# A two-layer memory-attention kernel: the last two segments projected as one, and other places for work in the one-layer steps

## The chip, the core and the metric

The kernel runs on one core of one Trainium2 chip. The metric is the device time of one execution in microseconds (us), the median of several runs. The core has a matrix engine (TensorE, PE in the profile; its weight loads are PEld), a vector engine (VectorE, DVE), a scalar engine (ScalarE, ACT), GpSimd (POOL) and a queue engine for transfers (SyncE, SP). Each engine works through a list of instructions of its own; semaphores join the lists. Matrix products land in the accumulation memory PSUM, from where DVE or ACT copies them into the main buffer.

## The reference

```python
# x: 2048 x 448; mem0: 8 x 448; 16 heads of 256; segments of 32 tokens
def _A_ref(x, mem0, Wq, Wk, Wv, Wo, seg_len):      # attention with a memory
    mem = mem0
    for s in range(n_seg):                          # 64 segments, in order
        h = concatenate([mem, x[segment s]])        # 8 + 32 tokens
        q, k, v = h @ Wq, h @ Wk, h @ Wv            # per head
        p = softmax(where(mask, q @ k.T * scale, -1e9))
        o = (p @ v) @ Wo
        mem = o[:M]                                 # the next segment's memory
        outs.append(o[M:])
def _B_ref(x, W_gate, W_up, W_down):                # feed-forward, 448 -> 1792 -> 448
    gate = x @ W_gate
    return (gate * (gate > 0) * (x @ W_up)) @ W_down
x = x + _A_ref(layernorm(x), ...)
x = x + _B_ref(layernorm(x), ...)
x = x + _A_ref(layernorm(x), ...)
x = x + _B_ref(layernorm(x), ...)
```

Both layers use the same weights. Each layer is a chain: a segment's memory is needed before the next segment's scores.

## The kernel before

**Preparation (to about 69 us).** The weights come in, are transposed on PE and multiplied out: A_sb holds the products of query and key weights, B_sb those of value and output weights. So a step needs no separate q, k, v or output product. `idle` (L322 to L329) adds 32 and 16 transposes of the identity that nothing reads.

**Steps.** `step(g, ff)` (L599 to L838) runs for g = 0 to 68. It holds segment g of layer 1 (chain c = 0, g up to 63) and segment g - 4 of layer 2 (c = 1, g from 4 to 67). So steps 0 to 3 and 64 to 67 have one chain, the "one-layer steps", and 60 steps have two. A step's stages, by the names in the profile:

- prj: hT (the normalized tokens and memory, transposed) times A_sb, into PSUM banks that `open_banks` and `close_bank` (L508 to L546) open and copy to TQ and TZ, the queries. Heads come in two halves, hf = 0 and 1; the banks are named b0 to b3 with z0 and z1 for the first half, c0 to c3 for the second.
- Sm and Sx: scores of the memory's 8 queries (`scores_m`, L621) and of the 32 tokens (`scores_x`, L629). `weights_begin` and `weights_end` (L554 to L571) turn them into probabilities PM and PX: mx, se, ssum, rs on DVE with the exponential on ACT.
- flips: PE transposes the probabilities, pps in whole (`flipped`, L573) or ppr in row halves (`flipped_rows`, L581), and DVE (ACT for one half of the rows) copies them to PT.
- weighting: `weigh_m` (L644, products ya and yb) for the memory's first half, `weigh_m_rows` (L657, ym) for its second, `weigh_x` (L673, y) for the tokens. The results go to Y (first half of the heads) and Z (second half). The memory's are used in the same step, the tokens' in the next.
- projection: `project_out` (L703) multiplies B_sb with Y and Z into one PSUM bank ox, 168 matmuls a step; `project_tail` (L714) does the last 64 output dimensions in 56 matmuls o, in column pairs, rows 0 to 63 and 64 to 127 of one bank. So step g projects the memory of step g and the tokens of step g - 1. Step 68 has no chain and only projects the tokens of segment 63 of layer 2. `finish` (L736) copies ox into the next memory and into OT, the tokens' output.

**Feed-forward.** The class `Feed` (L408 to L478) handles a block of 64 tokens of layer 1 (rows 64 to 127) and one of layer 2 (rows 0 to 63) at once. It runs at odd g from 3 on, 33 times inside a step, and once after the loop (L852 to L859). In steps 3 and 5 there is no layer-2 block yet; in step 67 and after the loop no layer-1 block is left. Its parts: `residual` (flips OT to otp, adds, statistics), `norm` (rstd on POOL, then xn; L769 asks for POOL, after the loop DVE does it), `xposed` (four transposes tps, copies to xT), `gate_up(u)` for u = 0 to 6 (28 matmuls ups and gps each, ut on ACT, hh on DVE), `down` (14 matmuls dps and the add), `norm2` and `feed_on` (the normalized block goes to layer 2) and `leave` (layer 2's block is stored).

**What sets the order.** The order on PE is written by hand: `mm`, `tr` and `in_order` (L71 to L85) tie each matmul to the one before in program order. The orders of DVE, ACT, POOL and SP follow from a scheduler. The pool "ps" has seven PSUM banks, handed around by all tags; ox has the eighth. A matmul that opens a bank waits for the reader of its former content.

In a one-layer step the middle goes like this (L793 to L800), before `project_out` fills the time in which the probabilities are made:

```python
            Sx0 = scores_x(0)
            if ff is not None:
                ff.xposed()
            scores_m(1)
            Sx1 = scores_x(1)
            pm = flipped(PM[0], 1, "m0")
            weigh_m(0, hk, pm)
            probs_x(0, Sx0)
```

Of the kernel before, what the change touches and what calls it, by code (L numbers as in the profile page):

```python
# [8 lines left out]
BF = mybir.dt.bfloat16  # L9
# [44 lines left out]
def build_kernel(ctx, tc, A_x, A_mem0, A_Wq, A_Wk, A_Wv, A_Wo, B_W_gate, B_W_up, B_W_down, out,  # L54
# [29 lines left out]
    def tr(*a):  # L84
        in_order(nc.tensor.transpose(*a))  # L85
# [119 lines left out]
        nc.vector.tensor_copy(mem_cols(g, cs)[:, 0:n], src)  # L205


    with tc.tile_pool(name="pre", bufs=3) as pre:
        mem0_n = pre.tile([MEM, 512], BF, name="mem0_n", bufs=1)
        nc.gpsimd.dma_start(mem0_n[:, 0:DM], mem0)  # L210
# [108 lines left out]
            load_next()  # L319
            return transposed(nat[i], i == 0)  # L320

        warm = psum.tile([P, 2 * DM], BF, tag="ps", name="warm")  # L322
        def idle(n):
            for _ in range(n):
                tr(warm[:, 0:128], ident[:], ident[:])

        idle(32)
        cur = flip_next(0)
        idle(16)  # L329
# [67 lines left out]
    nc.vector.memset(OT[:], 0.0)  # L397
    xT = main.tile([P, NPASS, 128], BF, name="xT")
    hh = main.tile([P, FT, 128], BF, name="hh")
    nc.gpsimd.memset(hh[:], 0.0)  # L400
    HK = []
    for i in range(2):
# [5 lines left out]
    class Feed:  # L408


        def __init__(self, i):
            self.i = i
            self.first = i < nblk
            self.second = 0 <= i - LAG // BLK < nblk
            self.n = slice(0 if self.second else TB, P if self.first else TB)
            self.x = xa[i % 3]
            self.nx = xp[i % 2]

        def residual(self):
            tp = flipped_dims("otp", lambda r, kd: OT[ROWS[r], kd, :])  # L420
# [7 lines left out]

        def xposed(self):
            tps = transpose_tokens(self.xn)  # L430
            nc.vector.tensor_copy(xT[:, 0:4, :], tps[:])
            for r in range(2):
                nc.scalar.copy(xT[ROWS[r], 4:NPASS, :], tps[ROWS[1 - r], 0:3, :])  # L433

        def gate_up(self, u):
            n = self.n
# [13 lines left out]
        def down(self):  # L450
            i = self.i
            dps = self.dps = psum.tile([P, 512], F32, tag="ps", name="dps")
            for f in range(FT):
                mm(dps[:, 0:DM], hh[:, f, :], Wd_sb[:, f, :], start=(f == 0), stop=(f == FT - 1))
            if self.first:
                nc.vector.tensor_tensor(self.nx[TB:P, :], dps[TB:P, 0:DM], self.x[TB:P, :], op=ALU.add)
                self.st = row_stats(self.nx)
                nc.sync.dma_start(xa[(i + 2) % 3][0:TB, :], self.nx[TB:P, :])
                if i + 3 < nblk:
                    nc.sync.dma_start(self.x[TB:P, :], x_dram[block(i + 3)])  # L460

        def norm2(self):
            if self.first:
# [4 lines left out]
        def leave(self):  # L468
            i = self.i
            if self.second:  # L470
                nc.vector.tensor_tensor(self.x[0:TB, :], self.dps[0:TB, 0:DM], self.x[0:TB, :], op=ALU.add)
                nc.sync.dma_start(out_dram[block(i - LAG // BLK)], self.x[0:TB, :])

        def feed_on(self):
# [103 lines left out]
        nc.vector.tensor_copy(PT[:], pps[:].rearrange("p b q -> p (b q)"))  # L578
        return PT

    def flipped_rows(srcs):  # L581

        blocks = [src[:, 2 * b:2 * b + 2, :] for src, n in srcs for b in range(n)]
        n = len(blocks)
        two = [psum.tile([P, n, 64], BF, tag="ps", name=f"ppr{r}") for r in range(2)]
        for b, src in enumerate(blocks):
            for r in range(2):
                tr(two[r][:, b, :], src[ROWS[r]], ident[ROWS[r], ROWS[r]])
        PT = main.tile([P, n * 128], BF, tag=f"PTr{n}", name="PT")
        for r, eng in enumerate((nc.vector, nc.scalar)):  # L590
            evac(eng, PT[:].rearrange("p (b r q) -> p b r q", r=2, q=64)[:, :, r, :], two[r][:])
        return PT

# [5 lines left out]
    def step(g, ff):  # L599
# [4 lines left out]
        hb = hTb[gb % 2]  # L604
        cols = [(0, 32) if c == 0 else (48, 80) for c in xs] + [(32, 40) if c == 0 else (40, 48) for c in ms]
        lo, hi = min(a for a, _ in cols), max(b for _, b in cols)
        ox = None

        def ys(hf, later=0):
# [62 lines left out]

        def weigh_x(hf, hk, PT):  # L673

            def keep(eng, c, t0, src):
                n = src.shape[-1] // SEG
                dst = ys(hf, 1)[:, t0:t0 + n, XO[c]:XO[c] + SEG]
                k = max(1, n // 8)
                evac(eng, dst.rearrange("p (k i) (e q) -> p k e i q", k=k, q=16),
                     src.rearrange("p (k e i q) -> p k e i q", k=k, e=2, q=16))  # L680

            y1 = {c: psum.tile([P, 512], F32, tag="ps", name=f"y1_{c}") for c in chains}
            for kd in range(2):
                for c in chains:
                    rows = slice(64 * c, 64 * c + L)
                    mm(y1[c][:, kd * 256:kd * 256 + 256], hk[rows, kd, :], PT[rows, 0:256], start=True, stop=True)
            for c in chains:
                keep(nc.scalar if c == 0 else nc.vector, c, 0, y1[c][:])
            y2 = {c: psum.tile([P, 512], F32, tag="ps", name=f"y2_{c}") for c in chains}
            for kd in (2, 3):  # L690
                for c in chains:
                    rows = slice(64 * c, 64 * c + L)
                    mm(y2[c][:, kd * 256 - 512:kd * 256 - 256], hk[rows, kd, :], PT[rows, 0:256], start=True, stop=True)
            for c in chains:
                keep(nc.scalar if c == 0 else nc.vector, c, 16, y2[c][:, 0:256])
                tail = y2[c][:, 256:512].rearrange("p (o e i q) -> p e i o q", o=2, e=2, i=4)
                for e in range(2):
                    rows = slice(64 * e, 64 * e + 64)
                    evac(nc.vector if c == 0 else nc.scalar,
                         ys(hf, 1)[rows, 24:28, XO[c]:XO[c] + SEG].rearrange("p i (o q) -> p i o q", q=16),  # L700
                         tail[rows, e])

        def project_out(hf, t0, t1):  # L703

            nonlocal ox
            if ox is None:
                ox = psum.tile([P, 3, W], F32, tag="ox", bufs=1, name="ox")
            for t in range(t0, t1):
                for mc in range(3):
                    mm(ox[:, mc, lo:hi], B_sb[:, hf, t, mc * 128:(mc + 1) * 128],  # L710
                       ys(hf)[:, t, lo:hi], start=(hf == 0 and t == 0 and mc == 0),
                       stop=(hf == 1 and t == NT - 1 and mc == 2), skip_group_check=True)

        def project_tail():  # L714

            o3 = psum.tile([P, W], F32, tag="ps", name="o3")
            for hf in range(2):
                for t in range(0, NT, 2):
                    for e in range(2):
                        mm(o3[64 * e:64 * e + 64, lo:hi], B_sb[:, hf, t + e, 384:DM], ys(hf)[:, t + e, lo:hi],  # L720
                           start=(hf == 0 and t == 0), stop=(hf == 1 and t == NT - 2))
            nc.scalar.copy(swap[0:64, lo:hi], o3[64:128, lo:hi])
            nc.scalar.copy(swap[64:128, lo:hi], o3[0:64, lo:hi])
            if ms:
                both = slice(M0 + MEM * ms[0], M0 + MEM * (ms[-1] + 1))
                nc.vector.tensor_tensor(mem_cols(g + 1, ms)[:, 3], o3[:, both].rearrange("p (c m) -> p c m", m=MEM),
                                        swap[:, both].rearrange("p (c m) -> p c m", m=MEM), op=ALU.add)
            for c in xs:
                x = slice(XO[c], XO[c] + SEG)
                nc.vector.tensor_tensor(ot_cols(c)[:, 3], o3[:, x], swap[:, x], op=ALU.add)  # L730

        def ot_cols(c):
            o = (g - 1) % BLK * SEG + (TB if c == 0 else 0)
# [2 lines left out]
        def finish():  # L736
            if ms:
                src = ox[:, :, M0:M0 + 16].rearrange("p k (c m) -> p k c m", m=MEM)
                set_mem(g + 1, src[:, :, ms[0]:ms[-1] + 1, :], ms, 3)
            for c in xs:  # L740
                nc.scalar.copy(ot_cols(c)[:, 0:3], ox[:, :, XO[c]:XO[c] + SEG])

        def feed(*us):
            if ff is not None:
# [21 lines left out]
        close_bank(b2, chains, hb, j, nc.scalar)  # L766
        if ff is not None:
            ff.residual()
            ff.norm(nc.gpsimd)  # L769
        b1, b3, z0, z1 = open_banks(chains, hb, j, (0, 1), (0, 3), (0, 4), (1, 4))  # L770
        close_bank(z0, chains, hb, j, None)
        load_some()
# [6 lines left out]
        close_bank(c0, chains, hb, j, nc.scalar)  # L779
        close_bank(c2, chains, hb, j, nc.scalar)  # L780
        close_bank(c1, chains, hb, j, nc.vector)
        close_bank(c3, chains, hb, j, nc.scalar)
        if len(chains) == 2:
            pm = flipped(PM[0], 1, "m0")
# [6 lines left out]
            probs_x(0, Sx0)  # L791
        else:
            Sx0 = scores_x(0)  # L793
            if ff is not None:
                ff.xposed()
            scores_m(1)
            Sx1 = scores_x(1)
            pm = flipped(PM[0], 1, "m0")
            weigh_m(0, hk, pm)
            probs_x(0, Sx0)  # L800
        if g < 2:
            load_some()
        if ff is not None:
# [47 lines left out]

    ff = Feed(nblk + LAG // BLK - 1)  # L852
    ff.residual()
    ff.norm()
    ff.xposed()
    for u in range(FT // 2):
        ff.gate_up(u)
    ff.down()
# [59 lines left out]
```

## Time and profile before

| what | value |
|---|---|
| median of 3 runs | 1584.73 us (1580.89, 1584.73, 1585.72) |
| the profiled execution | 1579.01 us, its span 1576.9 us |
| PE busy | 1547.3 us, 98% of the span |
| PEld, DVE, ACT, POOL busy | 90%, 71%, 50%, 11% |
| mean granted clock of TensorE | 0.993 |
| ACT copies OT <- ox | 128, 24.8 us |
| DMA | 33.12 MB, mean 21 GB/s |

The profile's page is one execution as the hardware profiler saw it. It gives each engine's busy time, then the span in 40 slices with tenths of busy time and of the granted clock, then the chain of waits that ended last, then groups of instructions. A group's line names the source line, the engine, the operation, output <- input, the shape and the count; then come busy us and mean ns of one, and behind the second bar the idle us of the engine just before them with what ended it. PE's mean ns is one instruction's latency, and neighbours overlap; a rate comes from busy us over the count. The timeline's lines give start and duration in us and, in brackets, the wait before. Counts of the form 128*64 are rows times columns of the matrix engine in use.

### The profile page before, as it was taken

The numbers are of one execution on the slowest core, as the hardware profiler recorded it, in microseconds if no ns is written. First come the engines' busy times: TensorE is split into PE (matmuls) and PEld (weight loads), VectorE is DVE, ScalarE is ACT, GpSimd is POOL, SyncE is SP. The second block draws the span as 40 slices with busy tenths as digits, with TensorE's granted clock in tenths as the row PEclk, the third lists the DMA queues.
The fourth block names the chain that finished last, engine by engine and source line by source line (L and its number), as shares of the span: only waits on it lengthen the run. The fifth ranks groups of instructions, "written<-read, shape, count | busy, mean of one in ns | idle before, by whom it ended". The sixth has DMA issues, their size and how long they took to land.

```text
span 1576.9 us, 98176 instructions
## 1 busy us (share of the span) xinstructions
PE 1547.3 (98%) x45116; PEld 1422.8 (90%) x45116; DVE 1112.7 (71%) x3825; ACT 783.3 (50%) x2307; POOL 174.9 (11%) x308
## 2 busy tenths in 40 slices
PE   8999999999999999999999999999999999999997
PEld 6588899999999999999999999999999999999886
DVE  6756777777777777777767677776777777776673
ACT  6634544554445544544445545554455545544442
POOL 3201111011001111011001111011011110111010
PEclk9989999999999999999999999999999999999999
DMA  9530000000000000000000000000000000000000
GB/s 285 149 80 9 9 10 8 6 10 10 10 10 10 10 10 8 6 9 10 10 10 10 10 10 5 8 10 10 10 10 10 10 10 5 9 8 7 7 7 6
DMA packets 29468, 33.12 MB, mean 21 GB/s; under 512 B 3320, under 2 KB 28160, under 8 KB 29056
## 3 DMA queue, kind: packets, MB, share of 16 engines
q1 hardware_dynamic: 28992, 26.85, 6.3%
q8 instruction: 352, 5.77, 1.5%
q14 instruction: 60, 0.49, 0.1%
q0 software_dynamic: 64, 0.01, 0.0%
HBM read 23.18 MB, written 1.84 MB: 16 GB/s over the span
## 4 chain that ended last, share of the span: by engine, by line
PE 94%; DVE 2%; ACT 1%; POOL 1%; issue 1%; DMA 0%; SPq 0%; POOLq 0%; ACTq 0%; DVEq 0%
PE prj L82 29%; PE ox L82 25%; PE ups L82 10%; PE dps L82 6%; PE o L82 5%; PE y L82 4%; PE Sx L82 3%; PE Sm L82 2%; PE bps L82 1%; PE pps L85 1%; PE gps L82 1%; PE aps L82 1%; PE tps L85 1%; PE kps L85 1%; PE ym L82 1%
## 5 line engine op out<-in xcount | busy, mean ns | idle before, releaser
L82 PEld LDWEIGHTS <-B_sb 128*128 128x128 bf16 (+1 forms) x15456 | 495.0, 103 | 29.2 <-issue 21.2
L82 PE MATMUL prj<-hT,A_sb 128*128 128x80 bf16 (+1 forms) x11424 | 430.6, 200 | 0.0
L82 PEld LDWEIGHTS <-A_sb 128*128 128x128 bf16 x11424 | 406.3, 100 | 8.3
L82 PE MATMUL ox<-Y,B_sb 128*128 128x80 bf16 (+4 forms) x5880 | 222.9, 199 | 1.9 <-DVE Y L650 1.9
L89 ACT CAST TQ<-prj 128x480 bf16<-128x480 f32 (+1 forms) x380 | 183.1, 494 | 82.8 <-PE prj L82 58.6
L82 PE MATMUL ox<-Z,B_sb 128*128 128x80 bf16 (+2 forms) x5712 | 217.7, 199 | 1.3 <-DVE Z L650 1.3
L82 PE MATMUL ups<-xT,Wgu_sb 64*128 64x128 bf16 (+1 forms) x3332 | 190.8, 214 | 1.3 <-DVE hh L447 0.8
L82 PE MATMUL gps<-xT,Wgu_sb 64*128 64x128 bf16 (+1 forms) x3332 | 190.9, 214 | 0.4 <-ACT xT L433 0.3
L82 PEld LDWEIGHTS <-Wgu_sb 64*128 64x128 bf16 x6664 | 179.1, 95 | 4.5 <-issue 2.5
L91 DVE CAST TQ<-prj 128x480 bf16<-128x480 f32 (+1 forms) x228 | 129.5, 574 | 17.3 <-PE prj L82 11.7
L447 DVE SCALAR_TENSOR_TENSOR hh<-gps,ut 128x256 bf16<-128x256 f32 (+1 forms) x238 | 94.7, 408 | 47.7 <-ACT ut L446 34.7
L446 ACT CAST ut<-ups 128x256 bf16<-128x256 f32 (+1 forms) x238 | 85.5, 359 | 82.1 <-PE gps L82 63.4
L89 ACT CAST Y<-y 64x128 bf16<-64x128 f32 (+2 forms) x256 | 89.4, 379 | 45.6 <-DVE Y L91 41.4
L91 DVE CAST Y<-y 64x128 bf16<-64x128 f32 (+2 forms) x256 | 102.1, 419 | 13.3 <-ACT Y L89 4.3
L89 ACT COPY hT<-tps 128x256 bf16<-128x256 bf16 x32 | 11.9, 372 | 197.8 <-DVE hT L91 197.8
L91 DVE CAST Z<-y 64x128 bf16<-64x128 f32 (+2 forms) x256 | 99.1, 418 | 12.4 <-ACT Z L89 5.5
L578 DVE COPY PT<-pps 128x128 bf16<-128x128 bf16 (+1 forms) x206 | 49.9, 256 | 80.3 <-PE pps L85 77.6
L89 ACT CAST Z<-y 64x128 bf16<-64x128 f32 (+2 forms) x256 | 89.2, 378 | 23.9 <-DVE Z L91 17.4
L89 ACT CAST TZ<-prj 64x320 bf16<-64x320 f32 (+2 forms) x152 | 56.1, 380 | 86.7 <-DVE TZ L91 78.7
L171 POOL TENSOR_SCALAR rstd<-mv 128x1 f32<-128x1 f32 x67 | 15.2, 227 | 729.2 <-DVE mv L169 729.2
L566 DVE TENSOR_REDUCE ssum<-se 128x2 f32<-128x80 f32 (+1 forms) x270 | 70.8, 274 | 35.7 <-ACT se L560 33.5
L82 PE MATMUL dps<-Wd_sb,hh 128*128 128x448 bf16 x476 | 96.0, 353 | 0.0
(130 smaller groups left out, 2342.1 us busy)
## 6 DMA issues: line engine op xcount, KB each, us to landing
wo<-in_A_Wo_dram SPq DMA_DIRECT2D x8, 448.0 KB, 7.7
nat<-in_A_Wq_dram SPq DMA_DIRECT2D x8, 384.0 KB, 6.2
nat<-in_A_Wk_dram SPq DMA_DIRECT2D x8, 384.0 KB, 6.4
nat<-in_A_Wv_dram SPq DMA_DIRECT2D x8, 384.0 KB, 7.2
xa<-in_A_x_dram SPq DMA_DIRECT2D x32, 56.0 KB, 2.8
xa<-xp SPq DMA_DIRECT2D x32, 56.0 KB, 1.9
out_dram<-xa SPq DMA_DIRECT2D x32, 56.0 KB, 2.0
xp<-in_A_x_dram SPq DMA_DIRECT2D x30, 56.0 KB, 2.1
```

The costliest lines, as they stand in the source:

```text
L82: in_order(nc.tensor.matmul(*a, **k))
L85: in_order(nc.tensor.transpose(*a))
L89: nc.scalar.copy(dst, src)
L91: eng.tensor_copy(dst, src)
L171: nc.gpsimd.tensor_scalar(out=rstd[:], in0=mv[:, 1:2], scalar1=EPS, scalar2=None, op0=ALU.add)
L446: nc.scalar.copy(ut[:, :, n], ups[:, :, n])
L447: nc.vector.scalar_tensor_tensor(out=hh[:, 2 * u:2 * u + 2, n], in0=gps[:, :, n], scalar=0.0, in1=ut[:, :, n], op0=ALU.max, op1=ALU.mult)
L566: nc.vector.tensor_reduce(ssum[:], se[:], axis=AX.X, op=ALU.add)
L578: nc.vector.tensor_copy(PT[:], pps[:].rearrange("p b q -> p (b q)"))
```

## The change

Parts, in the order of the diff:

1. `idle` becomes a function that takes a PSUM bank of its own at each call; the 32 and 16 transposes of the preparation stay. After the loop `idle(44)` stands between `residual` and `norm`, `idle(12)` between `xposed` and `gate_up`.
2. `xposed` copies only the 64 token columns that exist when the block has one half.
3. `down` for such a block (steps 3, 5, 67 and after the loop) takes 64 columns of hh as weights and writes even f to rows 0 to 63 and odd f to rows 64 to 127 of dps. `sum_up` then adds the two halves and x: a copy on ACT and two adds on DVE, instead of one add.
4. `weigh_x` in step 67 writes segment 63's y beside segment 62's, into the same buffers. Step 67 then projects nothing and only feeds, flips and weighs; step 68 projects 64 columns, both segments at once. 224 matmuls (168 ox, 56 o) are gone.
5. `finish` copies the second segment's OT on DVE instead of ACT. This holds in all 60 two-layer steps too, and once in step 68.
6. In one-layer steps `norm` runs on DVE; the memory flip `pm` comes right behind the first `scores_x`, `weigh_m` between `scores_m(1)` and the second `scores_x`, and `xposed` between the closes of banks c1 and c3. In step 67 there is no memory flip.

In the built kernel's lists, PE has 15232 loads of B_sb (15456 before), 56 dps matmuls of 64 rows beside 420 of 128 (476 before) and 104 idle transposes (48). DVE has 61 copies OT <- ox (0) and ACT 67 (128). In the two-layer steps the OT copy stands on DVE behind the first copy of y. In steps 3 and 65 DVE's list has both xn ahead of the last queries' copies TQ of bank b1, for which the memory scores Sm of the first half wait. Two early loads change places on SP. PE's list in the two-layer steps is the same.

```diff
+    def idle(n):
+        warm = psum.tile([P, 128], BF, tag="ps", name="warm")
+        for _ in range(n):
+            tr(warm[:], ident[:], ident[:])
...
+            self.both = self.first and self.second
...
         def xposed(self):
             tps = transpose_tokens(self.xn)
-            nc.vector.tensor_copy(xT[:, 0:4, :], tps[:])
+            n = self.n
+            nc.vector.tensor_copy(xT[:, 0:4, n], tps[:, :, n])
             for r in range(2):
-                nc.scalar.copy(xT[ROWS[r], 4:NPASS, :], tps[ROWS[1 - r], 0:3, :])
+                nc.scalar.copy(xT[ROWS[r], 4:NPASS, n], tps[ROWS[1 - r], 0:3, n])
...
             for f in range(FT):
-                mm(dps[:, 0:DM], hh[:, f, :], Wd_sb[:, f, :], start=(f == 0), stop=(f == FT - 1))
+                if self.both:
+                    mm(dps[:, 0:DM], hh[:, f, :], Wd_sb[:, f, :], start=(f == 0), stop=(f == FT - 1))
+                else:
+                    mm(dps[ROWS[f % 2], 0:DM], hh[:, f, self.n], Wd_sb[:, f, :], start=(f < 2), stop=(f >= FT - 2))
...
+        def sum_up(self, dst, o):
+            n = slice(o, o + TB)
+            if self.both:
+                nc.vector.tensor_tensor(dst[n, :], self.dps[n, 0:DM], self.x[n, :], op=ALU.add)
+                return
+            nc.scalar.copy(part[n, 1, :], self.dps[TB - o:P - o, 0:DM])
+            nc.vector.tensor_tensor(part[n, 0, :], self.dps[n, 0:DM], self.x[n, :], op=ALU.add)
+            nc.vector.tensor_tensor(dst[n, :], part[n, 0, :], part[n, 1, :], op=ALU.add)
...
+        last = g == nseg + LAG - 1
+        now = 0 if chains else 1
+        if not chains:
+            lo -= SEG
+
+        def outs():
+            if not chains:
+                return [(lo, OT[:, :, SEG:TB]), (lo + SEG, OT[:, :, 0:SEG])]
+            return [(XO[c], ot_cols(c)) for c in xs]
...
+            kept, xo = (ys(hf), (None, XO[1] - SEG)) if last else (ys(hf, 1), XO)
...
-            for c in xs:
-                nc.scalar.copy(ot_cols(c)[:, 0:3], ox[:, :, XO[c]:XO[c] + SEG])
+            for k, (x, ot) in enumerate(outs()):
+                evac(nc.vector if k else nc.scalar, ot[:, 0:3], ox[:, :, x:x + SEG])
...
-            ff.norm(nc.gpsimd)
+            ff.norm(nc.gpsimd if len(chains) == 2 else None)
...
         close_bank(c1, chains, hb, j, nc.vector)
+        if ff is not None and len(chains) == 1:
+            ff.xposed()
         close_bank(c3, chains, hb, j, nc.scalar)
...
             Sx0 = scores_x(0)
-            if ff is not None:
-                ff.xposed()
+            pm = flipped(PM[0], 1, "m0") if ms else None
             scores_m(1)
+            weigh_m(0, hk, pm)
             Sx1 = scores_x(1)
-            pm = flipped(PM[0], 1, "m0")
-            weigh_m(0, hk, pm)
             probs_x(0, Sx0)
+        if last:
+            probs_x(1, Sx1)
+            feed(0, 1, 2, 3)
+            px0 = flipped_rows([(PX[0], 2)])
+            feed(4)
+            weigh_x(0, hk, px0)
+            feed(5)
+            px1 = flipped_rows([(PX[1], 2)], "x1")
+            feed(6)
+            weigh_x(1, hk, px1)
+            ff.down()
+            ff.leave()
+            return
...
     ff.residual()
+    idle(44)
     ff.norm()
     ff.xposed()
+    idle(12)
```

More of the change, by code (lines that the diff above doesn't have):

```diff
@@ L320, in flip_next @@
             return transposed(nat[i], i == 0)
[L322 to L325, printed above, removed]
         idle(32)
@@ L399, in build_kernel @@
     hh = main.tile([P, FT, 128], BF, name="hh")
+    part = main.tile([P, 2, DM], F32, name="part")
     nc.gpsimd.memset(hh[:], 0.0)
@@ L453, in down @@
             for f in range(FT):
-                mm(dps[:, 0:DM], hh[:, f, :], Wd_sb[:, f, :], start=(f == 0), stop=(f == FT - 1))
+                if self.both:
+                    mm(dps[:, 0:DM], hh[:, f, :], Wd_sb[:, f, :], start=(f == 0), stop=(f == FT - 1))
+                else:
+                    mm(dps[ROWS[f % 2], 0:DM], hh[:, f, self.n], Wd_sb[:, f, :], start=(f < 2), stop=(f >= FT - 2))
             if self.first:
-                nc.vector.tensor_tensor(self.nx[TB:P, :], dps[TB:P, 0:DM], self.x[TB:P, :], op=ALU.add)
+                self.sum_up(self.nx, TB)
                 self.st = row_stats(self.nx)
@@ L470, in leave @@
             if self.second:
-                nc.vector.tensor_tensor(self.x[0:TB, :], self.dps[0:TB, 0:DM], self.x[0:TB, :], op=ALU.add)
+                self.sum_up(self.x, 0)
                 nc.sync.dma_start(out_dram[block(i - LAG // BLK)], self.x[0:TB, :])
@@ L579, in flipped, with flipped_rows @@
         return PT
-    def flipped_rows(srcs):
+    def flipped_rows(srcs, tag=""):
         blocks = [src[:, 2 * b:2 * b + 2, :] for src, n in srcs for b in range(n)]
@@ L588, in flipped_rows @@
                 tr(two[r][:, b, :], src[ROWS[r]], ident[ROWS[r], ROWS[r]])
-        PT = main.tile([P, n * 128], BF, tag=f"PTr{n}", name="PT")
+        PT = main.tile([P, n * 128], BF, tag=f"PTr{n}{tag}", name="PT")
         for r, eng in enumerate((nc.vector, nc.scalar)):
@@ L673, in weigh_x @@
         def weigh_x(hf, hk, PT):
+            kept, xo = (ys(hf), (None, XO[1] - SEG)) if last else (ys(hf, 1), XO)
             def keep(eng, c, t0, src):
                 n = src.shape[-1] // SEG
-                dst = ys(hf, 1)[:, t0:t0 + n, XO[c]:XO[c] + SEG]
+                dst = kept[:, t0:t0 + n, xo[c]:xo[c] + SEG]
                 k = max(1, n // 8)
@@ L699, in weigh_x @@
                     evac(nc.vector if c == 0 else nc.scalar,
-                         ys(hf, 1)[rows, 24:28, XO[c]:XO[c] + SEG].rearrange("p i (o q) -> p i o q", q=16),
+                         kept[rows, 24:28, xo[c]:xo[c] + SEG].rearrange("p i (o q) -> p i o q", q=16),
                          tail[rows, e])
@@ L710, in project_out @@
                     mm(ox[:, mc, lo:hi], B_sb[:, hf, t, mc * 128:(mc + 1) * 128],
-                       ys(hf)[:, t, lo:hi], start=(hf == 0 and t == 0 and mc == 0),
+                       ys(hf, now)[:, t, lo:hi], start=(hf == 0 and t == 0 and mc == 0),
                        stop=(hf == 1 and t == NT - 1 and mc == 2), skip_group_check=True)
@@ L719, in project_tail @@
                     for e in range(2):
-                        mm(o3[64 * e:64 * e + 64, lo:hi], B_sb[:, hf, t + e, 384:DM], ys(hf)[:, t + e, lo:hi],
+                        mm(o3[64 * e:64 * e + 64, lo:hi], B_sb[:, hf, t + e, 384:DM], ys(hf, now)[:, t + e, lo:hi],
                            start=(hf == 0 and t == 0), stop=(hf == 1 and t == NT - 2))
@@ L727, in project_tail @@
                                         swap[:, both].rearrange("p (c m) -> p c m", m=MEM), op=ALU.add)
-            for c in xs:
-                x = slice(XO[c], XO[c] + SEG)
-                nc.vector.tensor_tensor(ot_cols(c)[:, 3], o3[:, x], swap[:, x], op=ALU.add)
+            for x, ot in outs():
+                nc.vector.tensor_tensor(ot[:, 3], o3[:, x:x + SEG], swap[:, x:x + SEG], op=ALU.add)
         def ot_cols(c):
@@ L739, in finish @@
                 set_mem(g + 1, src[:, :, ms[0]:ms[-1] + 1, :], ms, 3)
-            for c in xs:
-                nc.scalar.copy(ot_cols(c)[:, 0:3], ox[:, :, XO[c]:XO[c] + SEG])
+            for k, (x, ot) in enumerate(outs()):
+                evac(nc.vector if k else nc.scalar, ot[:, 0:3], ox[:, :, x:x + SEG])
         def feed(*us):
```

## The prediction

> **What bounds the kernel now.** I read the table of slices first, then the chain of waits, then PE's waits by line, then the end in order of time. From the page:
>
> ```profile
> PE   8999999999999999999999999999999999999997
> PEclk9989999999999999999999999999999999999999
> ...
> PE 94%; DVE 2%; ACT 1%; POOL 1%; issue 1%; DMA 0%; SPq 0%; POOLq 0%; ACTq 0%; DVEq 0%
> ...
> L82 PE MATMUL dps<-Wd_sb,hh 128*128 128x448 bf16 x476 | 96.0, 353 | 0.0
> ```
>
> TensorE is busy at full clock in every slice but the last, and 94% of the chain is its own work. Here time goes only if matmuls go or if PE waits less. The last line's 96.0 us over 476 is 200 ns for a down matmul (the 353 beside it is one instruction's latency), so the 14 of one block take 2.8 us. Where PE waits, by its groups:
>
> ```profile
> L82 PE MATMUL ya<-PT,hk 128*128 128x128 bf16 x134 | 18.2, 217 | 2.7 <-DVE PT L578 2.7
> ...
> L82 PE MATMUL ox<-Z,B_sb 128*128 128x40 bf16 x504 | 14.4, 180 | 1.3 <-DVE Z L650 1.3
> ```
>
> With 1.9 us of the same kind for `ox<-Y`, and 0.5 us at `pps`, these are the one-layer steps: seven stalls of 0.43 to 0.54 us before ya and seven of 0.50 to 0.62 us before ox. In the two-layer steps PE hardly waits. The end, in order of time:
>
> ```profile
> 1556.41 4.38 PE L82 MATMUL ox<-Y,B_sb 128*128 128x32 bf16 x168
> ...
> 1561.12 0.29 PE L85 MATMUL otp<-ident,OT 64*128 64x64 bf16 x8 [0.33 <-ACT OT L741]
> ...
> 1564.24 0.61 PE L85 MATMUL tps<-ident,xn 128*128 128x128 bf16 x4 [2.82 <-DVE xn L181]
> ...
> 1565.35 0.97 ACT L433 COPY xT<-tps 64x384 bf16<-64x384 bf16 x2 [4.28 <-DVE xT L431]
> ...
> 1570.35 2.82 PE L82 MATMUL dps<-Wd_sb,hh 128*128 128x448 bf16 x14
> 1573.20 0.62 DVE L471 TENSOR_TENSOR xa<-dps,xa 64x448 bf16<-64x448 f32 x1 [2.21 <-PE dps L82]
> ```
>
> The last segment's projection and the last feed-forward block stand alone here. In this stage the granted clock is 1.00 until 1562, 0.57 in 1562 to 1564.2, 0.50 until 1569 and 0.95 after. So gate-up takes 4.85 us (1565.37 to 1570.2).
>
> **The change part by part.** Base: the profiled execution, 1579.01 us (span 1576.9 and 2.1 around it), 5.7 under the median of 1584.73. I subtract the sum from both.
>
> *End, steps 67 and 68.* Removed from step 67: 168 ox matmuls of 32 columns at 26.5 ns (4.45 us) and 56 o at about 22 ns (1.23 us). Step 68's ox grows to 64 columns: 40 columns cost 27.5 ns and 80 cost 36, between them about 32, so 168 x 5.5 ns = +0.9. Its o tail costs 20 to 22 ns at any width shown: 0. Down in pairs: 14 matmuls in 7 slots of 200 ns, -1.4. Work: -4.45 - 1.23 + 0.9 - 1.4 = -6.2. PE's waits in 1539 to 1556.4 are 0.31 + 0.27 + 0.65 + 0.93 + 0.26 = 2.4 us. The removed projection covered the softmax, the Z copies and the hh products; now only gate-up (28 matmuls of 64 columns, 0.41 us a call) and flips stand between them. With the order of the changed build I put its durations behind each other: the second scores wait 0.3 for queries on ACT; gate-up calls 3 and 4 wait 0.5 each for ut and hh; y waits 0.3 for its flip, the second y 1.0, since ACT copies a flip only behind the Z tails. That is 2.6, so -6.0. Bounds: all waits hidden, -8.6; each y copied with nothing beside it (Z copies 1.02 + 0.53, twice, 3 more), -3.0.
>
> *Last block.* OT is now copied for two segments, ACT (0.24) then DVE, which waits for ACT: +0.27. idle(44) runs while residual and norm run; a warm transpose took 55 ns at the start, so 2.4 of the 2.82 us wait is filled. idle(12), 0.66 us, lies beside the xT copies. xT narrower: DVE 0.43 to about 0.27; ACT's two 0.97 to about 0.6. At full clock the 196 gate-up matmuls take 14.7 ns (0.41/28). The first 17 need DVE's half, ready 0.16 earlier; the others wait for ACT until 0.6 after, and 179 x 14.7 = 2.6 more: 3.3 against 4.85 from a start 0.16 earlier, -1.7. Pairs -1.4. The sum of two halves is serial: ACT copy (0.53, the row of the 128x448 copy), DVE add, DVE add (about 0.6): +1.1. Sum -1.7; if the clock drops all the same, -0.4; if ACT's copies hide, -2.8.
>
> *Other down projections* (steps 3 and 5). Step 5: -1.4, and the chain of sum, statistics and xn, 1.1 longer, still ends where DVE reached xn before (185.71, rstd done at 184.43, tps at 186.54). Step 3: -1.4, but there xn (143.62) followed rstd (143.37) at once and tps at 144.06 had no slack: +0.8. The pairs' price is bounded by 0 (no overlap) and -1.4; I take -1.4, since in the preparation four aps matmuls of half width (128*64, 384 columns) last 0.52 us together, from 20.62, and two of full width 0.49, from 20.14: two halves in the time of one.
>
> [...]
>
> *norm on VectorE* (steps 3, 65; in 67 it removes the 0.31). In step 65 rstd ends at 1498.36 and PE starts the memory scores at 1498.50. In the changed order the two xn (0.40 each) stand ahead of the queries' TQ copy (0.23 to the first) that the scores need: 1498.36 + 0.80 + 0.23 = 1499.4, PE waits 0.9, and the chain behind is no shorter: +1.0. Step 3 the same (125.77 and 125.93): +1.0. Bounds 0 (PE's wait is made good by the flip and weighting behind it, which waited anyway) and +1.6 each (both TQ copies, 0.46, and a TZ copy come first as well). The four tps move ahead of one projection bank; they keep their 0.61 us and their xn is long there: 0. Narrower xT copies in steps 3, 5, 65 and 67 lie beside PE's work: 0.
>
> *Flip and weighting moved* in one-layer steps: the flip's DVE copy now stands behind Sx0, so ya's 0.5 us wait moves, but the 0.6 us wait before ox needs ya and yb copied, which end as late as VectorE's queue allows. I take 0 in steps 0 to 2 and 66 and -0.3 in 64. Bounds: half of 1.1 gone in each, -2.8; +0.3 each, +1.5.
>
> *OT copy on VectorE* in the 60 two-layer steps, 0.22 us each. It stands behind y1's copy, when ACT's is done. In an odd step DVE's last Z copy ends at 651.80 and PE opens the bank at 652.18: 0.38 us of cover. I take 0; that cover gone, rival 3. The other bound is 60 x -0.05 (ACT is freed of a copy). On SP's list two early loads change places and each output store follows its sum; past the weights no PE wait is for a DMA: 0.
>
> Sum: -6.0 - 1.7 - 1.4 (step 5) + 0.4 (step 3: 1.0 - 1.4 + 0.8) + 1.0 (step 65) - 0.3 = -8.0. On the profiled execution 1571.0; on the median **1576.7 us**.
>
> **Rivals.**
> 1. *Step 67 becomes bound by the vector engines.* Against it: PE waited only 2.4 us there and the DVE was half busy (8.1 of 17.1 us). For it: each engine runs its list in order, and the cover removed is 5.7 us. Price: end -3.0 instead of -6.0, total -5: 1579.7.
> 2. *The clock falls in step 67 or stays low at the end.* For it: in before it fell at about 1562.3, only 0.9 us after the last flips, with PE 1.2 us idle in the 3 us before it, and came back 4.8 us after PE went on. Waits of 1.0 and 0.5 us now lie close together. Against it: 1546 to 1548 stayed at 1.00 with a 0.93 us wait. Price: 4.8 us at half clock cost 2.4, and 1.3 at the last block are lost: total -4.3, 1580.4. [...]
> 3. *Slower: VectorE's OT copy releases banks late, 60 times.* It decides once the push is over 0.38 us. If the copy (0.22) also waits 0.36 for ACT behind ACT's y copies (0.38 for its two before), the push is 0.58 and 0.2 us are lost in each: +12.0, total +4: 1588.7. Against it: ACT's OT copies come ahead of its y copies, at 650.03, and end before y1's on DVE.
> 4. *Pairs run in single file.* +1.4 four times, with step 3's 0.8 as it is: total -2.4, 1582.3. Against: aps above.
>
> **How the numbers follow.** Forecast 0.58 (own range 1573.5 to 1580); better than it, stalls hidden in the end and the one-layer steps, 0.08 (1571); rival 1: 0.13; 2: 0.08; 3: 0.07; 4: 0.06. A measurement of this kernel can tell about 0.3%, 4.75 us, so faster is under 1580.0. Faster: 0.55 of the forecast, 0.08, half of rival 1 and a third of 2, 0.72. Slower is rival 3: 0.08 with what lies beyond it. Same: 0.20. The range reaches from 1571 to rival 4 with the unknown price of step 65: 1583.
>
> **What would show it.** In the changed profile: B_sb loads 15232, a last ox of 168 at 64 columns that begins within a few tenths of the last y; 56 dps of 64x448 in about 1.4 us per 14; the granted clock at 1.00 through the last gate-up, which takes about 3.2 us; a PE wait of about 0.9 us before Sm in steps 3 and 65; a pair of two-layer steps at 44.46 us as before (POOL's hT copy at 647.73 and 692.19). Wrong: if that pair grows by more than 0.1 us, if waits in step 67 sum to over 4 us, or if the clock there is under 0.9.

## The result and the profile after

The changed kernel takes 1585.65 us (median of 20 runs, 1582.49 to 1588.31), the kernel before 1582.42 (20 runs, 1579.71 to 1586.19). The ratio is 1.0018, 95% interval 1.0011 to 1.0025: slower, by some 3 us (0.2%), where 8 us faster was forecast. The time lies above the range. The profiled executions, on which the rows below rest, have spans of 1582.4 and 1576.9 us, 5.5 apart.

The page of the changed kernel, the same rows as before:

```profile
PE   8999999999999999999999999999999999999997
...
PEclk9989999999999999999999999999999999999999
...
PE 89%; DVE 5%; ACT 3%; issue 1%; POOL 1%; DMA 0%; SPq 0%; POOLq 0%; DVEq 0%; ACTq 0%
```

The slices show no difference: PE is as busy as before (98% of the span in both) and its clock as high (mean granted clock 0.995, before 0.993). The chain shows where to look. PE's share of it fell from 94% to 89%, and VectorE and ScalarE hold 8% where they held 3%: they have come onto the path, all along the span. The view of PE's waits by releaser (columns: us in total, times, longest) names the place at once:

```profile
PE prj L82 <- ACT Z L89: 10.2, 29, 0.4
PE ya L82 <- DVE PT L593: 1.8, 7, 0.4
```

The first line isn't in the view of the kernel before at all: 29 times, PE waits to start a projection product until ScalarE has copied a piece of Z. The second is what remains of the one-layer steps' 2.7 us. By groups, the product is A3z, which opens bank z1:

```profile
L82 PE MATMUL prj<-hT,A3z 64*128 64x80 bf16 x480 | 24.0, 198 | 10.2 <-ACT Z L89 10.2
...
L82 PE MATMUL ox<-Z,B_sb 128*128 128x40 bf16 x504 | 14.4, 179 | 0.6 <-DVE Z L674 0.6
...
L82 PE MATMUL dps<-Wd_sb,hh 128*64 128x448 bf16 x56 | 6.1, 354 | 0.0
```

The other two lines are gains that came: the wait before ox fell from 1.3 to 0.6 us, and a down matmul of half width costs 6.1/56 = 109 ns, where a full one costs 96.0/476, about 200.

A step's length is read from one mark a step, the copy of hT on POOL at its start. From the marks of the two profiled executions:

| stretch | before | changed | difference | forecast |
|---|---|---|---|---|
| start to step 3 | 119.51 | 119.29 | -0.2 | 0 |
| steps 3 to 5 | 68.11 | 65.58 | -2.5 | -1.0 |
| steps 6 to 63 | 1289.78 | 1305.21 | +15.4 | 0 |
| step 64 | 14.64 | 14.15 | -0.5 | -0.3 |
| step 65 | 26.50 | 27.36 | +0.9 | +1.0 |
| step 66 | 13.44 | 13.21 | -0.2 | 0 |
| step 67 to the end | 44.92 | 37.60 | -7.3 | -7.7 |

So one row is far off, and it is the largest: an odd two-layer step with its neighbour took 15.54 + 28.92 = 44.46 us and takes 15.54 + 29.46 = 45.00, 29 times 0.54. (The long stretch, 28.92, runs from the mark of an odd step to that of the next even one.) Everything else together brought 9.9 us, against the 8.0 forecast. (Why steps 3 to 5 gained more than forecast is told further below.)

Here is one such step of the changed kernel in order of time, the lines that read the last y and open the next bank:

```profile
652.71 0.24 ACT L89 CAST OT<-ox 128x96 bf16<-128x96 f32 x1 [2.64 <-DVE hT L205]
652.83 0.69 DVE L91 CAST Z<-y 128x512 bf16<-128x512 f32 x1
652.85 0.87 ACT L89 CAST Z<-y 128x512 bf16<-128x512 f32 x2
653.43 0.25 DVE L91 CAST OT<-ox 128x96 bf16<-128x96 f32 x1
653.75 1.05 DVE L91 CAST Z<-y 64x128 bf16<-64x128 f32 x3
...
654.83 0.53 ACT L89 CAST Z<-y 64x128 bf16<-64x128 f32 x2 [1.11 <-DVE Z L91]
654.86 0.20 PE L82 MATMUL prj<-hT,A3z 64*128 64x80 bf16 x1
...
655.41 0.30 PE L82 MATMUL prj<-hT,A3z 64*128 64x80 bf16 x7 [0.35 <-ACT Z L89]
```

ScalarE copies its OT and two large pieces, then stands for 1.11 us, until VectorE is through. What it waits for is the last of VectorE's three: in the built order these are first y, OT, the two tails (64x128), second y (128x256), and ScalarE's own two tails come from the same y bank as VectorE's second copy and wait for it. They end at 655.36, and PE goes on at 655.41. (The bracket counts idle time alone, 0.35 us. From the start of the first A3z matmul to the start of the next it is 0.55 us, which is nearer to what the step loses.) In the kernel before, the order was first y, second y, tails:

```profile
650.14 1.66 DVE L91 CAST Z<-y 128x512 bf16<-128x512 f32 x4
650.29 1.44 ACT L89 CAST Z<-y 128x512 bf16<-128x512 f32 x4
...
652.18 0.31 PE L82 MATMUL prj<-hT,A3z 64*128 64x80 bf16 x8
```

There ScalarE's four went through without a wait and ended at 651.73, 0.45 us before PE asked for the bank. Laid on each other (this step's marks are at 650.41 and 647.73, so 2.68 us apart), ScalarE ends 655.36 - 651.73 - 2.68 = 0.95 us later: 0.45 are covered, and PE loses the rest, 0.5.

The end went as forecast:

```profile
1562.87 5.07 PE L82 MATMUL ox<-Z,B_sb 128*128 128x64 bf16 x168
...
1568.56 0.29 PE L85 MATMUL otp<-ident,OT 64*128 64x64 bf16 x8 [0.62 <-DVE OT L91]
1568.79 2.63 PE L85 MATMUL warm<-ident 128*128 128x128 bf16 x44
...
1571.67 0.44 PE L85 MATMUL tps<-ident,xn 128*128 128x128 bf16 x4 [0.25 <-DVE xn L181]
...
1572.47 0.65 ACT L436 COPY xT<-tps 64x192 bf16<-64x192 bf16 x2 [4.26 <-DVE xT L434]
```

PE's 2.82 us wait before tps is filled by transposes of the identity; the granted clock is 1.00 from 1568 to 1579, where it was 0.50 from 1562.3 to 1569 in the same stage before; and gate-up runs from 1572.71 to 1575.9, 3.2 us instead of 4.85.

### The profile page after: what moved, and what is told of

The parts are those of the page before. It is cut to its first block, busy times and chain, and to the rows that moved or that the text cites. A ratio compares the mean times of both kernels' runs of the same rounds, so it can differ in the third digit from the quotient of the medians.

```text
span 1582.4 us, 97826 instructions
## 1 busy us (share of the span) xinstructions
PE 1546.5 (98%) x44947; PEld 1421.4 (90%) x44947; DVE 1125.9 (71%) x3895; ACT 776.7 (49%) x2249; POOL 167.5 (11%) x302
## 3 DMA queue, kind: packets, MB, share of 16 engines
HBM read 23.18 MB, written 1.84 MB: 16 GB/s over the span
## 4 chain that ended last, share of the span: by engine, by line
PE 89%; DVE 5%; ACT 3%; issue 1%; POOL 1%; DMA 0%; SPq 0%; POOLq 0%; DVEq 0%; ACTq 0%
PE prj L82 26%; PE ox L82 24%; PE ups L82 10%; PE dps L82 6%; PE o L82 5%; PE y L82 3%; PE Sx L82 3%; ACT Z L89 2%; DVE Z L91 2%; PE Sm L82 2%; PE bps L82 1%; PE aps L82 1%; PE pps L85 1%; PE gps L82 1%; PE tps L85 1%
## 5 line engine op out<-in xcount | busy, mean ns | idle before, releaser
L82 PEld LDWEIGHTS <-B_sb 128*128 128x128 bf16 (+1 forms) x15232 | 489.7, 103 | 24.7 <-issue 17.3
L82 PE MATMUL ox<-Y,B_sb 128*128 128x80 bf16 (+3 forms) x5712 | 218.5, 199 | 0.6 <-DVE Y L674 0.6
L89 ACT CAST Y<-y 128x512 bf16<-128x512 f32 (+1 forms) x252 | 87.8, 377 | 75.5 <-DVE Y L91 72.4
L91 DVE CAST Z<-y 64x128 bf16<-64x128 f32 (+2 forms) x260 | 104.0, 422 | 13.7 <-ACT Z L89 5.1
L91 DVE CAST Y<-y 128x512 bf16<-128x512 f32 (+1 forms) x252 | 102.9, 419 | 13.8 <-ACT Y L89 4.3
L575 ACT ACTIVATE se<-se 128x80 f32<-128x80 f32 (+1 forms) x270 | 71.4, 298 | 54.1 <-DVE se L574 48.8
L82 PE MATMUL prj<-hT,A 64*128 64x80 bf16 (+1 forms) x3264 | 94.3, 196 | 1.0 <-ACT TQ L89 0.4
```

The source lines that it names most:

```text
L82: in_order(nc.tensor.matmul(*a, **k))
L89: nc.scalar.copy(dst, src)
L91: eng.tensor_copy(dst, src)
L575: nc.scalar.activation(se[:], se[:], AF.Exp, scale=SCALE)
```

## The experiments

There are three theories at this point. *Order*: the loss is the place of VectorE's second y copy behind its two tails, which the OT copy brought with it. *Copy time*: VectorE simply has 0.25 us more to do at a tight place. *Elsewhere*: OT has nothing to do with it. In the table of marks "odd" is the long stretch.

**1. OT back on ScalarE.**

```diff
-                evac(nc.vector if k else nc.scalar, ot[:, 0:3], ox[:, :, x:x + SEG])
+                evac(nc.vector if k and not chains else nc.scalar, ot[:, 0:3], ox[:, :, x:x + SEG])
```

> The changed kernel with one part undone: in the two-layer steps the second OT copy is on ScalarE again (in step 68 it stays on VectorE). If that copy is what lengthens each pair of two-layer steps from 44.46 to 45.00 us, the pair comes back to 44.46 and the kernel is about 15.5 us (29 x 0.535) faster than the changed one, near 1570, 0.8% under the kernel before. If the loss has another cause, the pair stays at 45.00 and the time near 1585.

Measured: 1571.05 us, ratio to before 0.9915 (0.9901 to 0.993). Odd 28.92, even 15.54, steps 6 to 63 1289.34. The whole 15.4 us come back, and the line of 29 waits is gone. *Elsewhere* falls.

**2. OT on VectorE alone**, in the kernel before.

```diff
-            for c in xs:
-                nc.scalar.copy(ot_cols(c)[:, 0:3], ox[:, :, XO[c]:XO[c] + SEG])
+            for k, c in enumerate(xs):
+                evac(nc.vector if k else nc.scalar, ot_cols(c)[:, 0:3], ox[:, :, XO[c]:XO[c] + SEG])
```

> The kernel before with this part alone: the second OT copy on VectorE in the two-layer steps. If the copy is the cause by itself, the pair is 45.00 us and the kernel 15.5 to 16 us slower than before, about 1598 (ratio 1.010). If it does harm only together with another part, the pair stays at 44.46.

Measured: 1600.08 us, ratio 1.0103 (1.0088 to 1.0118); odd 29.46, steps 6 to 63 1305.83. The part does the harm by itself. Its built order has the second y behind the tails too.

**3. OT on VectorE, second y ahead of the tails.** The order is tied without a semaphore, as PE's order is; `behind` is the helper that does it.

```diff
+            top = {}
+            for c in reversed(chains):
+                top[c] = keep(nc.scalar if c == 0 else nc.vector, c, 16, y2[c][:, 0:256])
             for c in chains:
-                keep(nc.scalar if c == 0 else nc.vector, c, 16, y2[c][:, 0:256])
...
+                    if c == 0 and len(chains) == 2:
+                        behind(r, top[1])
```

> The changed kernel, OT copy still on VectorE, with VectorE's order tied to first y, OT, second y, tails (the changed kernel has first y, OT, tails, second y). Theory order: ScalarE's tail copies wait for VectorE's second y copy, and PE's next bank for them; with the second y ahead of the two tails they end about 0.6 us sooner, 0.15 before PE needs the bank, so the pair is 44.46 to 44.55 and the kernel 13 to 15.5 us faster than the changed one. Theory copy time: VectorE's 0.25 us more is the price whatever the order, the pair stays at about 45.0 and the time near 1585.

Measured: 1570.38 us, ratio 0.9913 (0.9897 to 0.993); odd 28.92. One step in order of time:

```profile
650.78 0.25 DVE L90 CAST OT<-ox 128x96 bf16<-128x96 f32 x1
650.95 0.91 DVE L90 CAST Z<-y 128x256 bf16<-128x256 f32 x3
651.40 0.53 ACT L89 CAST Z<-y 64x128 bf16<-64x128 f32 x2 [0.33 <-DVE Z L90]
```

VectorE still copies OT, for the same 0.25 us. But the 128x256 copy is now the first of the three, ScalarE waits 0.33 instead of 1.11 us, and PE not at all. *Copy time* falls: with this order the copy costs nothing, as the forecast had it.

**4. Tails first, nothing added**: experiment 1 with the second y tied behind the tails.

```diff
+            ends = []
             for c in chains:
-                keep(nc.scalar if c == 0 else nc.vector, c, 16, y2[c][:, 0:256])
+                top = keep(nc.scalar if c == 0 else nc.vector, c, 16, y2[c][:, 0:256])
+                if c == 1 and len(chains) == 2:
+                    behind(top, ends[1])
```

> The first experiment's kernel (OT on ScalarE) with VectorE's order tied to first y, tails, second y, nothing added to VectorE. Theory order: the second y ends 0.5 us later than in the kernel before, ScalarE's tail copies end 0.2 us after PE needs the bank, the pair is about 44.66 and the kernel some 6 us slower than the first experiment's. Theory copy time: no loss, pair 44.46.

Measured: 1590.55 us, ratio 1.0046 (1.0029 to 1.0063), 19.5 us above experiment 1. The order alone does it, and does three times what was expected: a pair takes 45.14 us, where 44.66 was expected and 44.46 is what experiment 1 takes. One step:

```profile
654.76 0.88 ACT L89 CAST Z<-y 128x512 bf16<-128x512 f32 x2
655.67 1.05 DVE L90 CAST Z<-y 64x128 bf16<-64x128 f32 x3 [0.37 <-ACT Z L89]
...
656.75 0.53 ACT L89 CAST Z<-y 64x128 bf16<-64x128 f32 x2 [1.11 <-DVE Z L90]
...
657.33 0.30 PE L82 MATMUL prj<-hT,A3z 64*128 64x80 bf16 x7 [0.49 <-DVE TQ L90]
```

VectorE's tails come from ScalarE's y bank, so they in turn wait for ScalarE's second copy, 0.37 us. I had left that out. ScalarE has two OT copies again here (0.38 us for both), so it is later, VectorE's tails with it, and then ScalarE's own. The two engines wait for each other in turn. That would explain why the changed kernel, where one OT copy had moved away, did better than this; no run separates it.

Two things in these rows can mislead. The record puts PE's wait down to VectorE's copy TQ, which ended within 0.02 us of ScalarE's tails; by the code the bank that this product opens last held layer 2's second y, and TQ doesn't read it. And by the marks the even step grew (16.37 us) while the odd one shrank (28.77): the mark of an odd step itself came late, behind copies that wait in the same way. PE's own work shows where the time went: from one last y to the next it takes 17.98 us over an even step, as in experiment 1, and the whole loss lies in the odd one.

**9. Why only odd steps.** In the changed kernel VectorE's order is the same in the even steps, and ScalarE waits the same 1.11 us there, yet they keep 15.54 us. They have no residual, whose flip otp takes one of the seven banks. The experiment takes one there:

```diff
             ff.norm(nc.gpsimd if len(chains) == 2 else None)
+        elif len(chains) == 2:
+            flipped_dims("otp", lambda r, kd: OT[ROWS[r], kd, :])
```

> The changed kernel with eight transposes more in each even two-layer step, at the place where an odd step flips OT for its residual and like them into one bank of the seven and the ox bank; nothing reads them. Theory banks: the late ScalarE tails cost nothing in even steps only because one bank less is asked for there; with this one more, the even step grows from 15.54 to about 16.2 us (0.13 to 0.15 of transposes and 0.5 of wait before z1), as the odd step did. Rival: odd steps lose for another reason (statistics or residual on VectorE), and the even step grows by 0.15 only.

Measured: 1604.36 us (one run). Even 16.15 instead of 15.54, odd 29.46 as in the changed kernel. In the view of waits there are now two lines:

```profile
PE prj L82 <- ACT Z L89: 10.1, 29, 0.4
PE prj L82 <- ACT Y L89: 8.9, 29, 0.3
```

(In the even steps the view calls the tokens' copies Y.) One bank more, and the even steps wait as the odd ones do: 0.61 us longer, of which the transposes are 0.13 to 0.15. The odd steps of experiments 1 and 3 take the bank too, with early tails, and don't wait. So the loss needs two things: late tails on ScalarE, and a step that asks for one bank more before z1.

**5 to 8 and the last two: the other terms**, each on experiment 1's kernel, whose marks are: steps 3 to 5 66.89, step 65 27.37, step 67 to the end 37.52.

```diff
-            ff.norm(nc.gpsimd if len(chains) == 2 else None)
+            ff.norm(None if last else nc.gpsimd)
```

> The first experiment's kernel with the norm on GpSimd again in steps 3 and 65 (step 67 keeps VectorE). If VectorE's xn ahead of the queries' copies costs what the prediction's term says, step 65 comes back from 27.37 to about 26.4 us and step 3 is up to 1.0 us shorter. If that wait is covered, step 65 stays within 0.2 us of 27.37.

Measured: 1570.07 us (one run), step 65 27.27. Neither of the expected falls came (step 3 takes 25.56 us, 25.55 in experiment 1): in step 65, with the norm on GpSimd, the tps transposes, now earlier, wait for it (two waits, 0.5 us in all).

```diff
-    idle(44)
...
-    idle(12)
```

> The first experiment's kernel without idle(44) and idle(12) after the loop. If they hold the clock, it falls to 0.5 before the last gate-up, which takes 4.6 to 4.9 us instead of 3.2, and the stretch from step 67's start to the end (37.5 us) grows by 1.3 to 2.0. If the clock would have held anyway (the last projection is wider and dense), the stretch stays at 37.5 or is 0.2 shorter.

Measured: 1572.4 us (one run), the last stretch 39.77, 2.25 longer, a little more than expected. The granted clock, in the view of windows (columns: length, then each engine's busy us, the clock, the share of DMA and GB/s):

```profile
1556.50:1564.00 7.50, 5.79 (x199) 5.49 (x200) 2.39 (x9) 2.22 (x8) 0.71 (x2) 0.54 0.01 2
```

The clock is at half all through the last gate-up, although the projection ahead of it is wide and dense. With the idle transposes the clock holds: it is 1.00 through the last gate-up in the changed kernel and in experiments 1, 3, 5 and 7 to 11. Without them it is at half for most of it: 0.61 from 1565.37 to 1570.20 in the kernel before, 0.54 from 1584.50 to 1592.00 in experiment 2, and 0.54 in the row above.

```diff
-            self.both = self.first and self.second
+            self.both = True
```

> The first experiment's kernel with down in 14 matmuls of full width and one add everywhere (xT copies and hh stay narrow). If pairs cost half and the three-part sum costs 1.1 us where it is on the path: step 5 1.4 us longer, step 3 about 0.6, step 67 1.4, the part after the loop 0.3 (1.4 less 1.1); 3.7 in all. If pairs do not overlap: every stage equal or shorter.

Measured: 1573.48 us (one run). Step 5 27.11 instead of 25.72 (+1.4); step 3 +0.1 (0.4 without the waits put down to "issue", for which the profile shows no releaser); the down matmuls of the last block start 1.42 later, which is step 67's share, and its sum ends 1.54 later, so the block itself loses 0.1. The end lies 2.5 later: about 1.0 us more passes between the last store's start and the end (4.0 us, 3.0 in experiment 1), which nothing here explains. Steps 5 and 67 are as expected; step 3 (0.6 expected) and the block (0.3) come out smaller.

```diff
-        last = g == nseg + LAG - 1
-        now = 0 if chains else 1
-        if not chains:
-            lo -= SEG
+        last = False
+        now = 0
```

> The first experiment's kernel with the last two segments projected one after the other, in steps 67 and 68, step 67 in the order of the other odd steps. Pairs, idle and VectorE's norm stay. By the prediction's terms the stretch from step 67's start to the end grows from 37.5 to about 42.5 us (work 4.45 + 1.23 - 0.9 = 4.8 more, waits about equal, 0.27 less for the OT copies). By the rival that vector engines bound step 67, it grows by 2 to 3 only.

Measured: 1576.22 us (one run), the last stretch 43.39, 5.9 longer. About 5 was expected. Some of the 5.9 is the clock, 0.57 in 1554.4 to 1558.4 in this run, which by my estimate accounts for 1.7 us at most (4.0 x 0.43); so the merged projection is worth between 4.2 and 5.9 us, and the rival that vector engines bound step 67, with 2 to 3, falls.

**10.** xposed behind the first `scores_x` again, and **11.** that with GpSimd's norm:

```diff
-        if ff is not None and len(chains) == 1:
-            ff.xposed()
         close_bank(c3, chains, hb, j, nc.scalar)
...
             Sx0 = scores_x(0)
+            if ff is not None:
+                ff.xposed()
```

> The first experiment's kernel with xposed behind the first scores_x again, as in the kernel before, in steps 3, 65 and 67; norm stays on VectorE there. If the tps transposes that now stand ahead of the last projection bank are what delays step 65, it shrinks from 27.37 to about 26.9 (the 0.5 us wait of Sm for TQ stays), and in step 67 the 1.0 us wait of Sx for TQ goes, so the last stretch falls from 37.5 to about 36.8. If Sm's wait for VectorE is all of it, step 65 stays at 27.37.

> The first experiment's kernel with both undone: norm on GpSimd in steps 3 and 65, and xposed behind the first scores_x. Step 65 back to about 26.5 us, the last stretch about 36.8, in all some 1.5 us under the first experiment: ratio to before about 0.991.

Measured: 1567.42 us (one run) and 1570.43, ratio 0.9921 (0.9906 to 0.9936). Step 65 takes 27.22 with xposed back alone and 26.41 with both back; each of the two moves hides the other's cost. The last stretch stays at 37.44 and 37.50, where 36.8 was expected: the 1.0 us wait of Sx for TQ goes, and waits behind it take its place. Experiment 11 gains 0.96 in step 65 and lost 1.4 in step 66 (14.61 against 13.21), where the clock fell:

```profile
1524.00:1526.00 2.00, 1.39 (x40) 1.31 (x41) 1.70 (x10) 0.77 (x3) 0.00 (x0) 0.92 0.03 8
1526.00:1528.00 2.00, 2.00 (x59) 2.00 (x56) 1.39 (x9) 0.34 (x1) 0.00 (x0) 0.50 0.00 0
```

The intervals of experiments 1, 3 and 11 overlap; no order among them is shown. Each beats both kernels, by about 0.85% against before.

## Why the prediction was wrong, step by step

- **The OT copy on VectorE: wrong, and all of the error.** The step reads "It stands behind y1's copy, when ACT's is done. In an odd step DVE's last Z copy ends at 651.80 and PE opens the bank at 652.18: 0.38 us of cover. I take 0". It measured 15.4 us. The step priced the copy's 0.22 us against VectorE's own end, and for that the 0.38 us would have done (experiment 3). It left out that the built order had changed behind the copy as well, second y behind the tails, and that ScalarE's tails wait for the second y. (The list of the built order above the diff names the OT copy's new place and not this one.) The cover to read was ScalarE's (651.73 against 652.18), and what it had to bear was 0.95 us: OT's slot of 0.32 (653.43 to 653.75), the two tails, about 0.5, and small gaps.
- **The third rival** named the place, the 60 steps and nearly the size (+4 in all, 3.2 measured), with a chance of 0.07. Its mechanism was not the one: VectorE's OT copy followed its first y copy without a wait for ScalarE, and it was a change of order that made the bank late. Its reason against, that ScalarE's copies come early, was true and beside the point. It also counted 60 steps; 29 lost, since only odd steps ask for the bank that is late.
- **The end: right.** From step 67's mark to the OT copy behind the last ox it took 28.85 us before and 23.18 now, -5.7 against -6.0. The single waits were off: Sx 1.0 instead of 0.3, the second y 0.6 instead of 1.0, the hh wait one of 0.4 instead of two of 0.5. Their sum was near (2.5 against 2.6), which is in part luck, since the single errors cancelled. The last block, from the end of ox: 16.07 before, 14.42 now, -1.65 against -1.7. OT's second copy added 0.3 (forecast 0.27), the sum of halves took 1.8 instead of 0.62 (forecast +1.1, measured +1.2), idle is worth 2.25 (forecast 1.3 for the clock).
- **Pairs: right.** 109 ns instead of 200 each: two halves take 218 ns where one full matmul takes 200, 18 ns more a pair.
- **norm on VectorE, step 65: the size right, the cause only half.** Measured +0.9 for +1.0. PE did wait for Sm's queries, but 0.5 us and not 0.9, and undoing the norm alone brought 0.1, since xposed's new place needs the early norm. The two moves cost together what I gave to one; that xposed's move costs "0" was wrong.
- **Steps 3 to 5: right, once one kind of wait is set aside.** They gained 2.5 us for a forecast 1.0 in this execution, and other kernels here with these edits take 65.9 to 67.1 us. The spread is mostly in waits that the profile puts down to "issue", that is to nothing it shows: 1.7 us in the kernel before, 0.2 in the changed one, 1.6 in experiment 1. Without them the stretch takes 66.4, 65.4 and 65.3 us, a gain of 1.0 to 1.1. By steps, step 3 then lost 0.1 to 0.4 (forecast +0.4), and steps 4 and 5 together gained 1.2 (forecast 1.4). What makes these waits stays open.
- **Flip and weighting:** ya's waits fell from 2.7 to 1.8 us and those before ox from 3.2 to 1.2, but waits at Sm, pps and ym came up; steps 64 and 66 gained 0.5 and 0.2. The forecast was -0.3. (The prediction reads the stalls before as 0.43 to 0.54 and 0.50 to 0.62 us; the rows of the kernel before give 0.32 to 0.52 and 0.40 to 0.53.)

## What to carry to other kernels

When an instruction is moved to another engine, read the whole built order around it, not the one instruction's slot: for each neighbour that changed places, ask which engine waits for it. Cover has to be read on the engine that releases the resource last, and through the waits between the engines; two engines that copy pieces of each other's banks pass a delay back and forth (0.37 and 1.11 us in the step of experiment 4). A side effect of half a microsecond, 29 times in a loop, weighs more than a rebuilt end that happens once, so price what touches the loop first.

## What the runs showed of the hardware

The clock can fall in the end of one execution and not in another of the same code. Steps 67 and 68 are the same code in the changed kernel and in experiment 9, and in 12.00 us from 0.14 us behind step 67's mark PE was busy for 10.39 us in the one (1544.94 to 1556.94) and 10.41 in the other (1562.60 to 1574.60). In the changed kernel the clock held, at 1.00 until 1578.4; in experiment 9 it fell in step 67, and the last stretch took 40.14 us instead of 37.60:

```profile
1576.60:1578.60 2.00, 1.02 (x32) 0.81 (x30) 1.28 (x6) 1.18 (x5) 0.00 (x0) 0.97 0.03 8
1578.60:1580.60 2.00, 2.00 (x12) 0.92 (x12) 0.98 (x2) 0.52 (x2) 0.00 (x0) 0.50 0.00 0
```

From 1574.60 to 1578.60, at whose end it fell, PE was busy for 2.67 of 4.00 us, and for 3.08 in the same stretch of the changed kernel (1556.94 to 1560.94), where the clock was 1.00. So the prediction's second rival, a fall in step 67, did happen, in one of nine executions with the changed step 67 (the changed kernel and experiments 1, 3, 5 to 7 and 9 to 11). In experiment 2, whose steps 67 and 68 are those of the kernel before, the clock fell three times, in step 67, in the last projection and in the last block, and the last stretch took 48.32 us, where the kernel before, with one fall, took 44.92:

```profile
1565.50:1571.50 6.00, 5.52 (x76) 3.00 (x76) 0.42 (x3) 0.88 (x4) 0.00 (x0) 0.72 0.01 3
1576.50:1581.50 5.00, 4.74 (x178) 4.61 (x176) 0.19 (x1) 0.74 (x4) 0.00 (x0) 0.66 0.03 7
1584.50:1592.00 7.50, 6.05 (x201) 5.69 (x202) 2.70 (x9) 2.55 (x8) 0.16 (x1) 0.54 0.01 2
```

What sets off a fall stays open. Before the first of these three, PE had waited 1.2 us before o, its longest wait from 1553 to 1580, and was busy for 0.84 of 2.00 us from 1564.50 to 1566.50. Before the second it was busy for 1.98 of 2.00 us from 1574.50 to 1576.50 and for 1.74 in the next 2.00, in which the clock fell (0.85), and from 1578.50 to 1580.50 the clock was at 0.50. The end of this kernel, which holds several waits of 0.5 to 1 us, took 1.4 us (step 66 of experiment 11), 2.5 us (experiment 9) and 3.4 us (experiment 2) more in one profiled execution than in another. A difference of that size there is not to be read as an effect of the code without a look at the clock.
